# Another order of the outer products in a two-level Strassen-Winograd output stage

## The chip, the cores and the metric

The kernel runs on one core of a Trainium2 chip. The metric is the device time of one execution in microseconds (us); the time before is the median of four runs. A profile of one further execution shows what each engine did: TensorE (PE, with its weight loads as PEld), VectorE (DVE), ScalarE (ACT), GpSimd (POOL), and SyncE (SP), which issues most DMAs.

## The reference

Attention with a hash mask gives x of 3072 x 512 (4 batches x 768 rows, 8 heads x 64). Then a feed-forward block follows, and it is the second product of that block that the change is about:

```python
def _moe_ref(x, w_in, w_out):
    h = x @ w_in                                   # 3072 x 2048
    g = h * (1.0 / (1.0 + np.exp(-1.702 * h)))
    return (g @ w_out).astype(np.float32)          # 3072 x 512
```

All is fp32.

## The kernel before, in words

Attention comes first. Then `feed_forward` computes the hidden layer in a first stage (`hidden`, products of 128x512 at L724) and the outputs in a second stage, which ends the kernel.

Both stages use the Winograd form of Strassen's scheme: a product of 2x2 blocks with seven block products in place of eight, and sums before and after. The output stage uses it twice, one inside the other.

*Outer level.* The tokens lie in three blocks `sb` of 1024. For each block there are seven outer products, numbered 1 to 7, done in the order of the tuple `OUTER`. So the output stage has 3 x 7 = 21 steps, `steps_out`; step n works on `(sb, o)`. `LEFT[o]` names the piece of w_out (or of the sums of its quarters) that the outer product takes, and `RIGHT[o]` the piece of g, which the first stage has left in DRAM (`g_dram`). The result of a step is a tile m of 128 x 4 quarters x 256, kept in `ms[o]`; six places (`wholes`) are used in turn. Some results are added to earlier ones as they are formed: `acc` names the earlier product. Products 6 and 2 take product 1, 7 and 3 take 6, and 4 takes 7. Product 5 takes none; after it, two sums over whole tiles are queued in `pending`, m6 += m5 (L976) and m5 += m7 (L977), and the transposition of m5. Product 3 takes the new m6, so the first of the two sums is done ahead of it.

*Inner level.* `product_of_halves(n, acc, after)` does one step: seven inner products `product(i)`, each four fp32 matmuls (the profile has two records for each), accumulated over four chunks in one of eight PSUM banks (L836); ACT copies the first to u (L849) and the third to c12 (L852), VectorE adds the others (L840). The four quarters c11, c12, c21, c22 of the result form so: the corner c11 = P2 + u, v = P6 + u, c21 = P7 + v, c12 = P3 + v, then P5 is added to c22 and c12, and P4 to c21. Where there is an `acc`, four more adds come in.

*What is put between.* `after(at)` is called at four or five places of a step, and issues work on VectorE in the places that suit it: at 0 whatever waits in `pending`, at 1 to 3 the four sums over g that the next step needs (`g_sums`: t1, b12 in place, t2, t4, at L219 to L222). `inner_sums` forms the sums over the pieces of w_out on POOL; those for the outer steps 5 and 6 are done in the first block ahead of these steps, each behind a copy of one element (`mark`, L940), which makes POOL wait for the corner of the step before:

```python
if n in (5, 6):
    nc.gpsimd.tensor_copy(mark, ms[OUTER[n - 1]][0:1, 0, 0:1])
for f in {0: inner_sums(4), 5: inner_sums(5) + inner_sums(6)[:2], 6: inner_sums(6)[2:]}.get(n, []):
    f()
```

*The outputs.* Finished results are transposed by VectorE, quarter by quarter, into `ys[j]` (`turned(c, i, j, q0, q1)`, L816), and written to DRAM by `written` (L823): four DMAs for one ys, or for a half of it. `ys[0]` needs the products 2 and 4, `ys[1]` the products 5 and 3. While a step runs, SP fetches the pieces of g for steps to come (`fetch`, L791).

*Order.* On PE, VectorE, ACT and POOL, instructions run in the order in which the program issues them. The DMAs on SP's queue are put in order by the framework, and each waits there for its data and its buffer.

Of the kernel before, what the change touches and what calls it, by code (L numbers as in the profile page):

```python
# [38 lines left out]
def kernel(  # L39
# [17 lines left out]
    nc = tc.nc  # L57

    loader = [nc.sync]
# [93 lines left out]
    for x in (0x3FFFFFFF, 0xFF800000):  # L153
        m = const.tile([P, 1], U32, name=f"mask_{x:x}")
# [53 lines left out]
    def sums_a(eng, a11, a12, s3, a22, s1, s2, s4, a21=None):  # L208

        a21 = s3 if a21 is None else a21  # L210
        return [lambda: eng.tensor_tensor(s1, a21, a22, op=Alu.add),
                lambda: eng.tensor_tensor(s3, a11, a21, op=Alu.subtract),
                lambda: eng.tensor_tensor(s2, s1, a11, op=Alu.subtract),
                lambda: eng.tensor_tensor(s4, a12, s2, op=Alu.subtract)]
# [480 lines left out]
    def feed_forward(tag, late=()):  # L695
# [5 lines left out]

        LEFT = dict(zip(range(1, 8), (0, 1, 6, 3, 4, 5, 2)))
        RIGHT = dict(zip(range(1, 8), (0, 2, 3, 6, 4, 5, 1)))
        OUTER = (1, 2, 6, 7, 5, 3, 4)
        with ExitStack() as fctx:
            stage_ctx = fctx.enter_context(ExitStack())
            stage = stage_ctx.enter_context(tc.tile_pool(name=f"stage{tag}", bufs=2, side="right"))
# [4 lines left out]
            def bank():  # L712
                turn[0] += 1
                return sets[turn[0] % 8 // 6 if len(sets) > 1 else 0].tile([P, XT], F32, tag="p", name="product")
# [53 lines left out]
            def w_quarters(o):  # L768

                w = wqs[LEFT[o]]  # L770
                x = [w[:, i, F4 * j : F4 * (j + 1), :] for i in range(2) for j in range(2)]
                at = OUTER.index(o)
                if at == 0:
                    return x[0:2] + rooms[3:4] + x[3:] + rooms[0:3]
                return x + rooms[3 * at + 1 : 3 * at + 4]

            def inner_sums(at):

                if at == 0:
                    w = w_quarters(OUTER[0])  # L780
                    return sums_a(nc.gpsimd, *w, wqs[LEFT[OUTER[0]]][:, 1, 0:F4, :])
                return sums_a(nc.gpsimd, *w_quarters(OUTER[at])) if at < len(OUTER) else []

            steps_out = [(sb, o) for sb in range(n1) for o in OUTER]
            raw_g = [None, s_in[:, 0:2].rearrange("p i k f -> p (i k f)").rearrange("p (c t) -> p c t", t=XT)]
# [25 lines left out]
            def turned(c, i, j, q0, q1):  # L811

                for q in range(q0, q1):
                    h, k = divmod(q, 2)
                    y = ys[j].rearrange("p b (d r) -> p r b d", r=4)[:, 2 * i + h, k * (TH // 32) : (k + 1) * (TH // 32), :]
                    nc.vector.transpose(y, c[:, q].rearrange("p (b t) -> p b t", t=32))  # L816

            def written(sb, j, halves, queues):
                first, last = halves[0] * TH, (halves[-1] + 1) * TH
                for a in range(4):  # L820
                    t0 = (2 * sb + j) * XT
                    dst = out[t0 + first : t0 + last, a * P : (a + 1) * P].rearrange("(b t) d -> t b d", t=32)
                    queues[a % len(queues)].dma_start(out=dst, in_=ys[j][32 * a : 32 * (a + 1), first // 32 : last // 32, :])  # L823

            def product_of_halves(n, acc, after):

                sb, o = steps_out[n]
                wq, gq = w_quarters(o), g_quarters(n)
                m = wholes[n % len(wholes)]
                u, v = (gp.tile([P, TH], F32, tag=x, name=x, bufs=2) for x in ("u", "v"))  # L830
                c11, c12, c21, c22 = (m[:, i] for i in range(4))

                def product(i):
                    ps = bank()[:, 0:TH]
                    for c in range(F4):
                        nc.tensor.matmul(ps, wq[LEFT[i]][:, c, :], gq[RIGHT[i]][:, c, :], start=(c == 0), stop=(c == F4 - 1))  # L836
                    return ps

                def add(dst, x, y):
                    nc.vector.tensor_tensor(dst, x, y, op=Alu.add)  # L840

                def corner():
                    add(c11, product(2), u)
                    if acc is not None:
                        add(c11, c11, acc[:, 0])


                final = n + 1 == len(steps_out)
                nc.scalar.copy(u, product(1))  # L849
                if not final:  # L850
                    corner()
                nc.scalar.copy(c12, product(3))  # L852
                after(0)
                add(v, product(6), u)
                add(c21, product(7), v)
                if acc is not None:
                    add(v, v, acc[:, 1])
                    add(c22, c21, acc[:, 3])
                    add(c21, c21, acc[:, 2])
                add(c12, c12, v)  # L860
                after(1)
                p = product(5)
                add(c22, p, c21 if acc is None else c22)
                add(c12, p, c12)
                after(2)
                if final:
                    corner()
                    after(4)
                add(c21, product(4), c21)
                after(3)  # L870
                return m
# [14 lines left out]
            for sb in range(n1):  # L886
                for mt in range(MT):
                    n = sb * MT + mt
                    if n == 1:
# [12 lines left out]
                        steps = conversions(cv, cps, late + chunks)  # L902
# [31 lines left out]
            for n, (sb, o) in enumerate(steps_out):  # L934
                final = n + 1 == len(steps_out)
                if 0 < n and n + 1 < len(steps_out):
                    fetch(n + 1)
# [5 lines that stand above are left out]
                later_sums = g_sums(n + 1)  # L943
                m = wholes[n % len(wholes)]

                def after(at):
                    if at == 0:
                        while pending:
                            pending.pop(0)()

                    steps = [later_sums[at : at + 1]] if n == 0 else [[], later_sums[0:1], later_sums[1:2], later_sums[2:], []][at : at + 1]

                    if n + 2 >= len(steps_out):
                        turns = [lambda q=q: turned(m, int(final), int(not final), q, q + 1) for q in range(4)]
                        if final:
                            steps = [[[], [], [turns[1], turns[3]], [turns[2]], [turns[0]]][at]]
                        elif at == 3:
                            steps = [later_sums[2:3], turns[0:2], turns[3:4], later_sums[3:], turns[2:3]]
                    for f in sum(steps, []):
                        f()  # L960
                    if final and at in (2, 3):
                        written(sb, 0, (3 - at,), loader + [nc.scalar])
                    if n + 2 == len(steps_out) and at == 3:
                        written(sb, 1, (0, 1), loader + [nc.scalar])

                acc = {6: 1, 7: 6, 2: 1, 3: 6, 4: 7}.get(o)
                if o == 3:
                    pending.pop(0)()
                ms[o] = product_of_halves(n, None if acc is None else ms[acc], after)

                def flat(x):
                    return x.rearrange("p q t -> p (q t)")

                if o == 5:
                    m5, m6, m7 = (ms[i] for i in (5, 6, 7))
                    pending += [lambda a=m6, b=m5: nc.vector.tensor_tensor(flat(a), flat(a), flat(b), op=Alu.add),  # L976
                                lambda a=m5, b=m7: nc.vector.tensor_tensor(flat(a), flat(a), flat(b), op=Alu.add),  # L977
                                lambda a=m5: turned(a, 1, 1, 0, 4)]
                elif o in (2, 3) and n + 2 < len(steps_out):
                    pending.append(lambda a=ms[o], j=int(o == 3): turned(a, 0, j, 0, 4))  # L980
                    if o == 3:
                        pending.append(lambda sb=sb: written(sb, 1, (0, 1), loader))
                elif o == 4 and not final:
                    pending.append(lambda a=ms[4]: turned(a, 1, 0, 0, 4))
                    pending.append(lambda sb=sb: written(sb, 0, (0, 1), loader))
                yield
# [50 lines left out]
```

## Time and profile before

| | us |
|---|---|
| median of 4 runs | 869.91 (869.39 to 870.5) |
| the profiled execution | 869.08 |
| its span, from the first to the last instruction | 867.2 |
| PE busy in it | 856.8 |
| DVE busy in it | 719.2 |
| first matmul of the output stage | 604.38 |
| last matmul ends | 858.77 |
| last transposition on DVE ends | 860.88 |

A line of the timeline has the start in us, the time that it takes in us, the engine, the line of the program, the operation, what it writes from what it reads, shape, and how many instructions are merged in it; in brackets the idle time of the engine before it and what ended that. A line of the chain of work that ended last has the start, the time, and the engine with its line. PEclk is the granted clock of TensorE as a share of full speed (here 0.998 over the span). Offsets such as +3.08 in what follows are us from the first matmul of a step.

### The profile page before, as it was taken

How to read it: one execution, taken by the hardware profiler on the slowest of the kernel's cores; microseconds unless marked ns; L12 is line 12 of the kernel's file. 1: busy time of each engine (PE TensorE's matmuls, PEld its weight loads, DVE VectorE, ACT ScalarE, POOL GpSimd, SP SyncE). 2: the span in 40 equal slices, each digit the busy share in tenths (PEclk: the TensorE clock that was granted, in tenths of full speed). 3: DMA queues.
4: the chain of work that ended last, by engine and by line, in shares of the span. 5: the costliest groups of instructions: out<-in, count | busy, mean ns of one | idle time of the engine just before them, and what ended most of it. 6: DMA issues, size and time to landing. Idle time of an engine off the chain costs nothing.

```text
span 867.2 us, 13473 instructions
## 1 busy us (share of the span) xinstructions
PE 856.8 (99%) x4845; PEld 498.6 (57%) x4845; DVE 719.2 (83%) x1020; ACT 313.4 (36%) x519; POOL 313.5 (36%) x275
## 2 busy tenths in 40 slices
PE   9999999999999999999999999999999999999996
PEld 4444444444444444444444444444888888888885
DVE  4589999999999887778777778888888977897786
ACT  5866667776666642332233322332000000000000
POOL 4242234333223567664544334759904100000000
PEclk9999999999999999999999999999999999999999
DMA  5636645556552205556455555575844685467524
GB/s 133 98 55 108 103 84 85 85 97 118 97 99 60 60 2 195 187 190 216 170 197 190 189 188 195 196 253 179 304 158 153 201 248 196 165 204 243 194 98 100
DMA packets 169162, 132.10 MB, mean 152 GB/s; under 512 B 123616, under 2 KB 138112, under 8 KB 163712
## 3 DMA queue, kind: packets, MB, share of 16 engines
q1 hardware_dynamic: 166528, 129.70, 52.5%
q10 hardware_dynamic: 2560, 1.46, 0.8%
q8 instruction: 40, 0.66, 0.4%
q14 instruction: 34, 0.28, 0.1%
HBM read 79.69 MB, written 50.33 MB: 150 GB/s over the span
## 4 chain that ended last, share of the span: by engine, by line
PE 95%; DVE 3%; issue 0%; DMA 0%; ACTq 0%; ACT 0%; DVEq 0%
PE product L724 33%; PE product L836 26%; PE ps L432 18%; PE av L465 15%; PE dn L486 1%; PE hash L408 1%; DVE y L816 1%; DVE xT L840 1%; PE tp L366 1%; DVE t_x L840 0%; DMA k<-in_k_dram 0%; PE hash L373 0%; DVE t2a L221 0%; DVE raw_g L220 0%; DVE v L840 0%
## 5 line engine op out<-in xcount | busy, mean ns | idle before, releaser
L433 ACT ACTIVATE e<-ps 128x768 f32<-128x768 f32 x192 | 151.3, 812 | 25.6 <-PE ps L432 23.1
L432 PE MATMUL ps<-qT,kT 64*128 64x384 f32 x768 | 155.1, 482 | 0.0
L724 PE MATMUL product<-xT,w_in_sb 128*128 128x512 f32 x288 | 135.4, 592 | 0.0
L465 PE MATMUL av<-e,v 128*32 128x385 f32 x1536 | 128.0, 487 | 0.0
L440 POOL TENSOR_TENSOR acc<-e 128x768 f32<-128x768 f32 x32 | 51.8, 1617 | 193.7 <-ACT e L433 174.2
L732 ACT ACTIVATE c<-c 128x512 f32<-128x512 f32 x72 | 45.4, 630 | 186.7 <-issue 78.6
L724 PEld LDWEIGHTS product<-xT,w_in_sb 128*128 128x128 f32 x288 | 54.6, 190 | 69.0 <-issue 64.5
L465 PEld LDWEIGHTS av<-e,v 128*32 128x32 f32 x1536 | 48.5, 109 | 76.2 <-issue 74.6
L724 PE MATMUL product<-t_x,s_in 128*128 128x512 f32 x192 | 90.2, 592 | 0.0
L432 PEld LDWEIGHTS ps<-qT,kT 64*128 64x128 f32 x768 | 68.0, 187 | 38.5 <-issue 38.4
L219 POOL TENSOR_TENSOR v<-c,u 128x512 f32<-128x512 f32 x24 | 34.2, 1424 | 122.2 <-ACT c L732 122.2
L849 ACT COPY u<-product 128x256 f32<-128x256 f32 x21 | 7.8, 373 | 172.1 <-PE product L836 138.9
L432 PE MATMUL ps<-qf,kf 64*128 64x384 bf16 x384 | 62.8, 324 | 0.1
L724 PEld LDWEIGHTS product<-t_x,s_in 128*128 128x128 f32 x192 | 36.5, 190 | 45.9 <-issue 43.3
L441 POOL TENSOR_TENSOR acc<-acc,e 128x768 f32<-128x768 f32 x32 | 55.8, 1744 | 2.5
L446 DVE SCALAR_TENSOR_TENSOR acc<-e 128x768 f32<-128x768 f32 x32 | 47.7, 1490 | 5.1 <-ACT e L433 5.1
L724 PE MATMUL product<-t_x,w_in_sb 128*128 128x512 f32 x96 | 45.1, 592 | 0.0
L724 PE MATMUL product<-xT,s_in 128*128 128x512 f32 x96 | 45.1, 592 | 0.0
L432 PEld LDWEIGHTS <-kf 64*128 64x128 bf16 x384 | 18.9, 94 | 35.1 <-issue 7.4
L448 DVE TENSOR_TENSOR acc<-acc,e 128x768 f32<-128x768 f32 x32 | 34.3, 1072 | 3.3
L448 DVE TENSOR_TENSOR acc<-acc,acc 128x768 f32<-128x768 f32 x32 | 31.2, 974 | 6.3 <-POOL acc L441 3.2
L836 PE MATMUL product<-raw_g,xT 128*128 128x256 f32 x152 | 35.1, 379 | 0.0
(207 smaller groups left out, 1496.7 us busy)
## 6 DMA issues: line engine op xcount, KB each, us to landing
raw_g<-g_dram SPq DMA_DIRECT2D x22, 1024.0 KB
s_in<-g_dram SPq DMA_DIRECT2D x20, 1024.0 KB
g_dram<-c SPq DMA_DIRECT2D x72, 256.0 KB
g_dram<-t SPq DMA_DIRECT2D x48, 256.0 KB
raw<-in_moe_w_in_dram SPq DMA_DIRECT2D x16, 512.0 KB
raw<-in_moe_w_out_dram SPq DMA_DIRECT2D x16, 512.0 KB
v<-in_v_dram SPq DMA_DIRECT2D x32, 192.0 KB
g_dram<-u SPq DMA_DIRECT2D x24, 256.0 KB
```

What stands on the lines that cost most here:

```text
L219: return [lambda: eng.tensor_tensor(t1, b12, b11, op=Alu.subtract), lambda: eng.tensor_tensor(b12, b22, b12, op=Alu.subtract), lambda: eng ...
L366: nc.tensor.matmul(tp[D * j : D * (j + 1), i * P : (i + 1) * P], x[name][:, j, c * GT + i, :], ident, start=True, stop=True)
L432: nc.tensor.matmul(ps[:, j, 0:HS], a[hs, keys], m[hs, cols], start=not last, stop=last)
L433: nc.scalar.activation(es[c][:, kt, :, 0:HS], ps[:, :, 0:HS], Act.Exp, scale=1.0 / D**0.5)
L440: nc.gpsimd.tensor_tensor(acc, es[c][:, 0, :, 0:HS], es[c][:, 1, :, 0:HS], op=Alu.add)
L441: nc.gpsimd.tensor_tensor(acc, acc, es[c][:, 2, :, 0:HS], op=Alu.add)
L446: nc.vector.scalar_tensor_tensor(acc, e[0], T * TINY, e[1], op0=Alu.add, op1=Alu.add)
L448: nc.vector.tensor_tensor(acc, acc, x, op=Alu.add)
L465: nc.tensor.matmul(av[D * j + d : D * j + d + 32, :], vt[:, t, j, d : d + 32], es[c][:, t, j, :], start=(t == 0), stop=(t == T - 1))
L724: nc.tensor.matmul(ps, wq[LEFT[i]][:, kc, :], xq[RIGHT[i]][:, kc, :], start=(kc == 0), stop=(kc == K2 - 1))
L732: nc.scalar.activation(c, c, Act.Gelu_apprx_sigmoid)
L836: nc.tensor.matmul(ps, wq[LEFT[i]][:, c, :], gq[RIGHT[i]][:, c, :], start=(c == 0), stop=(c == F4 - 1))
```

## The change

The order of the outer products becomes 1, 2, 6, 7, 4, 5, 3. So product 3 is the last of a block, product 4 the fifth and 5 the sixth. In the last block, `ys[0]` (products 2 and 4) is transposed and written from `pending` in the step of product 5, as in the other blocks, and `ys[1]` in two halves in the last step.

The last step of all has its own order of the inner products: it was 1, 3, 6, 7, 5, 2, 4, and becomes 1, 2, 6, 7, 4, 5, 3, where c12 is formed by two adds from P5 + v and P3 and not by ACT's copy of P3. Its quarters are transposed as they are done: c11, c21, then the first half of the rows is written, then c22, c12 and the second half. The special treatment of the step before the last goes: it had transposed and written its own result within the step, partly on ACT's queue.

```diff
-        OUTER = (1, 2, 6, 7, 5, 3, 4)
+        OUTER = (1, 2, 6, 7, 4, 5, 3)
...
                 nc.scalar.copy(u, product(1))
+                corner()
                 if not final:
-                    corner()
-                nc.scalar.copy(c12, product(3))
+                    nc.scalar.copy(c12, product(3))
                 after(0)
                 add(v, product(6), u)
                 add(c21, product(7), v)
...
                     add(c21, c21, acc[:, 2])
+                if final:
+
+                    add(c21, product(4), c21)
+                    after(1)
+                    p = product(5)
+                    add(c22, p, c22)
+                    after(2)
+                    add(c12, p, v)
+                    add(c12, product(3), c12)
+                    after(3)
+                    return m
                 add(c12, c12, v)
                 after(1)
                 p = product(5)
                 add(c22, p, c21 if acc is None else c22)
                 add(c12, p, c12)
                 after(2)
-                if final:
-                    corner()
-                    after(4)
                 add(c21, product(4), c21)
                 after(3)
                 return m
...
-                    if n + 2 >= len(steps_out):
-                        turns = [lambda q=q: turned(m, int(final), int(not final), q, q + 1) for q in range(4)]
-                        if final:
-                            steps = [[[], [], [turns[1], turns[3]], [turns[2]], [turns[0]]][at]]
-                        elif at == 3:
-                            steps = [later_sums[2:3], turns[0:2], turns[3:4], later_sums[3:], turns[2:3]]
+                    if final:
+                        turns = [lambda q=q: turned(m, 0, 1, q, q + 1) for q in range(4)]
+                        steps = [[[turns[0]], [turns[2]], [turns[3]], [turns[1]]][at]]
                     for f in sum(steps, []):
                         f()
-                    if final and at in (2, 3):
-                        written(sb, 0, (3 - at,), loader + [nc.scalar])
-                    if n + 2 == len(steps_out) and at == 3:
-                        written(sb, 1, (0, 1), loader + [nc.scalar])
+                    if final and at in (1, 3):
+                        written(sb, 1, (at // 2,), loader + [nc.scalar])
...
-                elif o in (2, 3) and n + 2 < len(steps_out):
+                elif o in (2, 3) and not final:
                     pending.append(lambda a=ms[o], j=int(o == 3): turned(a, 0, j, 0, 4))
                     if o == 3:
                         pending.append(lambda sb=sb: written(sb, 1, (0, 1), loader))
-                elif o == 4 and not final:
+                elif o == 4:
                     pending.append(lambda a=ms[4]: turned(a, 1, 0, 0, 4))
                     pending.append(lambda sb=sb: written(sb, 0, (0, 1), loader))
```

## The prediction

> **What bounds the kernel now.** I read the page first: the span, the engines' shares, the chain that ended last by engine.
>
> ```profile
> span 867.2 us, 13473 instructions
> PE 856.8 (99%) x4845; PEld 498.6 (57%) x4845; DVE 719.2 (83%) x1020; ACT 313.4 (36%) x519; POOL 313.5 (36%) x275
> PE 95%; DVE 3%; issue 0%; DMA 0%; ACTq 0%; ACT 0%; DVEq 0%
> ```
>
> TensorE sets the time. The change takes no matmul away, so it can gain only where TensorE stands still, or behind its last matmul. The chain in order of time shows where, in the stage of the outputs:
>
> ```profile
> 681.13 1.14 DVE t2a L221
> 682.28 0.14 issue
> 682.41 160.83 PE product L836 x744
> ...
> 853.83 0.38 ACT u L849
> ...
> 860.25 0.63 DVE y L816
> ```
>
> At 682.41 TensorE has waited for the sum t2a; from there it runs without a break; from about 854 the chain is on VectorE. A product of halves (8 matmul records) takes 1.725 us, a step of seven 12.09 (822.35 to 834.43). The step that starts at 676.93 is followed by one at 689.39, 12.46 later: the stall is 0.37. It is the only one of that size: the other thirteen steps to 846.52 take 157.13, 12.087 each. The timeline shows a step's VectorE work, and the tail:
>
> ```profile
> 834.43 3.62 PE L836 MATMUL product<-s_in,xT 128*128 128x256 f32 x16
> 837.51 1.22 DVE L976 TENSOR_TENSOR t_x<-t_x,xT 128x1024 f32<-128x1024 f32 x1
> 838.65 0.42 DVE L840 TENSOR_TENSOR xT<-product,u 128x256 f32<-128x256 f32 x1
> 839.44 1.22 DVE L977 TENSOR_TENSOR xT<-xT,t_x 128x1024 f32<-128x1024 f32 x1
> 840.70 2.06 DVE L816 STREAM_TRANSPOSE y<-xT 128x256 f32<-128x256 f32 x4
> 842.57 0.44 DVE L840 TENSOR_TENSOR v<-product,u 128x256 f32<-128x256 f32 x1
> ...
> 854.24 0.42 DVE L840 TENSOR_TENSOR v<-product,u 128x256 f32<-128x256 f32 x1 [1.49 <-ACT u L849]
> 856.88 1.89 PE L836 MATMUL product<-t4g,w_out_sb 128*128 128x256 f32 x8
> 860.25 0.63 DVE L816 STREAM_TRANSPOSE y<-xT 128x256 f32<-128x256 f32 x1
> ```
>
> TensorE ends at 858.77, VectorE at 860.88: VectorE is late by 1.0 against the least possible (one add of 0.42 and one transpose of 0.63 behind the last matmul). Behind it the output's bytes drain (stretches of 1 us; the last two columns are DMA share and GB/s):
>
> ```profile
> 859.00:860.00 1.00, 0.00 (x0) 0.00 (x0) 0.97 (x3) 0.00 (x0) 0.00 (x0) 1.00 0.64 130
> 861.00:862.00 1.00, 0.00 (x0) 0.00 (x0) 0.00 (x0) 0.00 (x0) 0.00 (x0) 1.00 1.02 262
> 863.00:864.00 1.00, 0.00 (x0) 0.00 (x0) 0.00 (x0) 0.00 (x0) 0.00 (x0) 0.93 1.01 223
> 864.00:865.00 1.00, 0.00 (x0) 0.00 (x0) 0.00 (x0) 0.00 (x0) 0.00 (x0) 0.50 0.65 133
> ```
>
> The queues are full from about 859.3 to 864.7; the span ends 2.5 later.
>
> **Part 1: outer products 4, 5, 3 for 5, 3, 4.** Each step keeps its 56 matmul records, so TensorE's work is unchanged: 0. What moves is VectorE's work. Outer product 3 is the heavy step: L976, L977, four transposes and four more adds with the earlier product (acc). Before, the light 5 precedes it; after, 5 still does, but carries product 4's four transposes (2.06 by the row at 840.70). Cover: in the step from 822.35, product 5 before, VectorE waits 2.35 ahead of v and 1.30 ahead of the next add. After an acc step its corner add comes at +4.34 (826.69 against 822.35), so the transposes run from +4.7 to +6.75, before product 6 lets v start at +7.10. They cost nothing; without that cover they would cost up to 2.06 at VectorE. The heavy step then begins as now: L976 at +3.08 (837.51 against 834.43).
>
> In the first block the stall arises because the heavy step's predecessor is stretched by POOL: L219 takes 2.29 at 663.09 and L220 1.63 at 665.97, against 1.22 each elsewhere. POOL's sums of outer steps 5 and 6 follow a one-element copy (L940) that waits for the previous product's corner. That copy's first wait now includes an acc add (+0.45, from 657.58), its second loses L976 and an acc add (from 672.31 to about 671.4). So the stretched sums stay in the step from 652.75 to 664.84, but what follows is the light 5, not the heavy 3. Working through the DVE rows, t2a for the step from 676.93 is ready at about 679.7, needed at 682.1; the next heavy step gives its successor's t2a at 693.0, needed at 694.2. The stall goes: -0.37 (bounds: 0 if POOL's two remaining sums stretch other adds, -0.40 with the 0.03 at 633.73).
>
> GPSIMD Engine Reference of the Trainium skill, section 1 (Specifications), says that POOL shares its SBUF interface with VectorE, in contention with instructions that have two SBUF inputs. The rows at 663.09 and 665.97 agree; by this rule alone the two sums from 671.4 would stretch any two-input add they meet, 1 us or so each, an estimate from 2.29 less 1.22. Beside the transposes (one input) the row at 673.42 shows none: 2.07 against 2.06.
>
> DMA queue: product 4's write of y (four issues on SP, 3.38 to 3.42 in all at 686.29 and 696.61) moves from the next block's first step to step 5, past the fetch for two steps on. The second half of that fetch, issued at 673.67, would go at about 677 to 678; L219 reads it at about 688.4 (688.55 now). The nearest row: issued at 689.81 for a read at 698.90, 9.1 us, with no wait there. Here 10.4 remain: 0. If it were late, the price is bounded by one issue stretch, 3.4. Product 3's write then takes the place of product 4's in the next block's first step: 0.
>
> **Part 2: the next to last step.** Its own four transposes and its half of the output (four issues, two on ACT) go. They hold ACT from 840.1 to 853.74, which delays u (L849) to 853.83 and VectorE by 1.49. Now ACT copies u at about 848.3. That wait goes; what is late next is VectorE's own queue. Half of the last 2 MB (y0, 1 MB) now leaves from about 841 instead of 852.8.
>
> **Part 3: the last step.** It is now heavy: P1, P2, P6, P7, P4, P5, P3. VectorE enters at 846.52 + 3.08 = 849.60. Spacings from the rows above and the tail's rows: L976 1.14; corner 0.45 + 0.34; L977 1.26; four transposes 1.87; the corner's own transpose 0.48; v 0.53, c21 0.46, v 0.34, c22 and c21 0.80 (0.40 each), P4 0.45; transpose 0.48; P5 0.45 (its wait on the sum included), transpose 0.48, c12 0.45, P3 0.45, last transpose 0.63. The sum is 11.06: the end is at 860.7, against 860.88. No product is late: P4 is done at 855.2 and needed at 857.2, P3 at 858.6 and needed at 859.6. So -0.2 (bounds: -1.0 if VectorE kept up with TensorE; +1.3 if the step were entered like an acc step's corner, at +4.35).
>
> **Part 4: the drain.** 2 x 512 KB, as now; the first half goes after the second own transpose, about 858.4 (858.62 now), the second at 860.7 (860.91 now): the same gap of 2.3. The rest of the earlier 1 MB no longer sits in front. I take no more than the shift; the bound is the rate: 1 MB in 5.4 us now, 4.7 at the row's 223 GB/s, so -0.7. DMA: Bandwidth & Descriptors, section "Anatomy of one DMA", puts a fixed cost of about 2.0 us on a transfer, mostly the write's receipt. By it the end would follow only the last issue; the windows show full queues until 864.7, so the first half's issue counts as much.
>
> **Sum.** -0.37 - 0.2 - 0 = -0.55: span 866.65, the profiled execution 869.08 - 0.55 = 868.5. The median shown, 869.91, is 0.83 above the profiled execution: 869.3.
>
> **Rivals.**
> - *Slower: VectorE enters the last step late.* Place: v of the next to last step. If the 2.35 + 1.30 of waits there were used up, the 2.06 of transposes and the 1.27 between +4.35 and +3.08 would add up to 3.3 on a tail that has nothing to absorb it: +2.75, 872.7. It decides from 2.3 on. For it: the last step holds 11.1 us of VectorE work in a 12.09 step. Against: those waits stand in the profile.
> - *Faster: TensorE sets the tail.* If adds go closer than I chain them, the end is 858.4 + 1.05, -1.4 against 860.88, and with -0.5 of the drain 868.0.
> - *Nothing comes of it.* POOL's sums stretch the next step, the stall stays, and the last step ends where it did: between -0.2 and +0.9, about 870.2.
>
> **How the numbers follow.** A measurement of this kernel tells about 0.2% (1.74 us) from no change. Forecast (-0.2 to -1.4): 0.52, same. Nothing: 0.22, same. Faster rival: 0.15. Slower rival: 0.11. Together: faster 0.15, same 0.74, slower 0.11. The range leaves out most of the slower rival and half of the faster one: 868.0 to 870.8.
>
> **What would show it.** Right: steps of 12.09 throughout, no break of TensorE near 682; no wait of VectorE for ACT's u in the last step; y0 written from 841; VectorE's last transpose ends at 860.2 to 860.5, and 1.6 to 2.0 after TensorE. Wrong: a break of TensorE near 682 or 694, L976 in the last step later than +3.5, a gap between the adds of the last step that is longer than 0.6, or SP's fetch late for L219.

## The result, and the profile after

The changed kernel takes 870.59 us (median of 32 runs) against 869.87 for the kernel before (52 runs): 1.0010 of its time, 95% interval 1.0005 to 1.0015. The ratio is taken over all runs and is not the quotient of the two medians, which would be 1.0008. So the kernel is slower by 0.7 us, where -0.6 was forecast. The interval does not reach 1, though the move is under the 0.2% that the prediction took for the least that can be told. The profiled execution took 869.83, its span 868.0.

The page after (the span, the engines' busy times, and the chain that ended last by engine):

```profile
span 868.0 us, 13477 instructions
PE 856.9 (99%) x4845; PEld 498.3 (57%) x4845; DVE 720.4 (83%) x1020; ACT 313.1 (36%) x518; POOL 311.9 (36%) x275
PE 96%; DVE 3%; issue 0%; POOL 0%; DVEq 0%; POOLq 0%
```

TensorE's work is the same to 0.1 us; the page doesn't tell where the time went. The chain in order of time does (start, us, engine, line):

```profile
661.43 0.44 DVE t_x L840
...
662.31 1.42 DVE t_x L840
...
663.75 2.78 DVE t_x L840 x2
...
669.80 1.14 DVE t2b L221
670.94 0.14 issue
671.08 172.92 PE product L836 x800
```

Before, the chain left VectorE for TensorE at 682.41, behind t2a. Now it does so at 671.08, behind t2b, one step earlier. From there TensorE has no break any more: every later step takes 12.08 or 12.09. The timeline at that place, POOL included:

```profile
661.43 0.42 DVE L840 TENSOR_TENSOR t_x<-product,v 128x256 f32<-128x256 f32 x1 [1.30 <-PE product L836]
661.92 1.51 POOL L214 TENSOR_TENSOR w_in_sb<-xT,w_in_sb 128x512 f32<-128x512 f32 x1
662.23 2.90 DVE L840 TENSOR_TENSOR t_x<-t_x,xT 128x256 f32<-128x256 f32 x2
663.39 1.45 POOL L211 TENSOR_TENSOR w_in_sb<-xT 128x512 f32<-128x512 f32 x1
664.68 3.62 PE L836 MATMUL product<-s_in,xT 128*128 128x256 f32 x16
664.92 1.33 POOL L212 TENSOR_TENSOR xT<-xT 128x512 f32<-128x512 f32 x1
665.04 1.48 DVE L840 TENSOR_TENSOR t_x<-t_x,v 128x256 f32<-128x256 f32 x1
666.45 1.21 DVE L219 TENSOR_TENSOR t1b<-s_in 128x1024 f32<-128x1024 f32 x1
669.72 1.21 DVE L221 TENSOR_TENSOR t2b<-s_in,t1b 128x1024 f32<-128x1024 f32 x1
671.08 1.97 PE L836 MATMUL product<-t2b,w_in_sb 128*128 128x256 f32 x8 [1.05 <-DVE t2b L221]
678.06 3.62 PE L836 MATMUL product<-raw_g,xT 128*128 128x256 f32 x16
```

The same place in the kernel before, from the add of product 7 to the product that takes t2b:

```profile
661.59 0.42 DVE L840 TENSOR_TENSOR t_x<-product,v 128x256 f32<-128x256 f32 x1 [1.30 <-PE product L836]
667.85 1.21 DVE L221 TENSOR_TENSOR t2b<-s_in,t1b 128x1024 f32<-128x1024 f32 x1
670.02 1.89 PE L836 MATMUL product<-t2b,w_in_sb 128*128 128x256 f32 x8
```

Two adds that take 0.88 elsewhere take 2.90 beside POOL's sums, a third takes 1.48 in place of 0.42. Everything behind them on VectorE moves, and TensorE waits 1.05 for t2b, which was ready 0.96 before it was wanted (669.06 against 670.02) in the kernel before. The sixth step lasts from 664.68 to 678.06, 13.38, where 12.09 is usual: +1.29. The seventh has its usual length, so the old stall of 0.37 is gone. From the first matmul of the stage (604.21, 604.38 before) to that of the last step (847.27, 846.52 before) the balance is +0.92.

The tail, as offsets from the first matmul of the last step:

| | before | after |
|---|---|---|
| v starts | +7.72 | +8.62 |
| last transposition ends | +14.36 | +14.36 |
| span ends | +20.66 | +20.75 |

```profile
855.89 0.40 DVE L840 TENSOR_TENSOR v<-product,u 128x256 f32<-128x256 f32 x1
861.00 0.63 DVE L816 STREAM_TRANSPOSE y<-xT 128x256 f32<-128x256 f32 x1
```

VectorE does not wait for ACT's u any more (no bracket at v), but it gets to v later, with its own queue, and ends at the same distance. So the loss lies in the first block.

### The profile page after: what moved, and what is told of

It reads as the page before. It is cut to its first block, busy times and chain, and to the rows that moved or that the text cites. A ratio compares the mean times of both kernels' runs of the same rounds, so it can differ in the third digit from the quotient of the medians.

```text
span 868.0 us, 13477 instructions
## 1 busy us (share of the span) xinstructions
PE 856.9 (99%) x4845; PEld 498.3 (57%) x4845; DVE 720.4 (83%) x1020; ACT 313.1 (36%) x518; POOL 311.9 (36%) x275
## 4 chain that ended last, share of the span: by engine, by line
PE 96%; DVE 3%; issue 0%; POOL 0%; DVEq 0%; POOLq 0%
PE product L724 33%; PE product L836 26%; PE ps L432 18%; PE av L465 15%; PE dn L486 1%; PE hash L408 1%; DVE t_x L840 1%; DVE xT L840 1%; PE tp L366 1%; DVE y L816 1%; PE hash L373 0%; DVE t4g L222 0%; DVE raw_g L220 0%; DVE xT L979 0%; DVE t2b L221 0%
## 5 line engine op out<-in xcount | busy, mean ns | idle before, releaser
L219 POOL TENSOR_TENSOR v<-c,u 128x512 f32<-128x512 f32 x24 | 34.2, 1423 | 122.3 <-ACT c L732 122.3
```

The costliest lines, as they stand in the source:

```text
L219: return [lambda: eng.tensor_tensor(t1, b12, b11, op=Alu.subtract), lambda: eng.tensor_tensor(b12, b22, b12, op=Alu.subtract), lambda: eng ...
```

## The experiments

Theory A: POOL's sums behind the first mark stretch VectorE's adds in the fifth step; the new order has four more adds there (the acc adds), and t2b is late for the sixth step. Rival B: the four adds alone make it late. Rival C: the loss lies in the tail.

**Two of the six sums moved behind the second mark** (`e1_split`):

```diff
-for f in {0: inner_sums(4), 5: inner_sums(5) + inner_sums(6)[:2], 6: inner_sums(6)[2:]}.get(n, []):
+for f in {0: inner_sums(4), 5: inner_sums(5), 6: inner_sums(6)}.get(n, []):
```

> The changed kernel with one edit: of POOL's six sums that follow the first mark, the last two (for the seventh step) are put behind the second mark, so four stand there. Theory A (POOL's sums stretch VectorE's two-input adds of the fifth step, which the new order has more of, and t2b for the sixth step comes too late): without the two sums the two adds of c22 and c21 take under 1.8 us where they took 2.90, the add of c12 0.42 to 0.9 where it took 1.48, t2b is ready before TensorE wants it at about 669.9, TensorE's break of 1.05 is gone, and the time falls by 0.9 to 1.3 against the changed kernel: 869.3 to 869.7. Rival B (the three more adds alone make VectorE late, POOL adds little): the break stays at over 0.7, the time at 870.2 to 870.8. Rival C (the loss is in the last step's tail): the break may go, the time stays at 870.4 or more.

Measured: 869.38 against 870.02 for the kernel before measured beside it, ratio 0.9992 (0.9983 to 1.0000). Its timeline (the profiled execution was 3.5 us late before it came to this stage, so only distances count):

```profile
665.74 1.95 DVE L840 TENSOR_TENSOR t_x<-t_x,xT 128x256 f32<-128x256 f32 x2
667.61 0.42 DVE L840 TENSOR_TENSOR t_x<-t_x,v 128x256 f32<-128x256 f32 x1
671.21 1.21 DVE L221 TENSOR_TENSOR t2b<-s_in,t1b 128x1024 f32<-128x1024 f32 x1
673.37 1.89 PE L836 MATMUL product<-t2b,w_in_sb 128*128 128x256 f32 x8
```

t2b is ready at 672.42, 0.95 ahead of TensorE, and there is no break. The two adds took 1.95, a little over the 1.8 expected. The time is 1.36 lower than the changed kernel's, each against its own kernel before (-0.64 and +0.72), and the intervals of the two ratios do not meet. B and C fall: the acc adds and the new tail are all still there. The two sums that were moved do stretch VectorE in the sixth step (an add of 0.42 takes 0.98, L219 2.29), but there t2a is still ready at 683.82 and TensorE takes it at 685.46.

**One sum moved** (`e7_one_sum`; the same edit with `[:1]` and `[1:]`):

> The changed kernel, with five POOL sums behind the first mark in place of six (none moved: 1.05 break; two moved: t2b ready 0.95 ahead). Theory A, each sum costs VectorE the time for which it holds the common reads, about 1.0 us: t2b comes within 0.3 of the time at which TensorE wants it, so a break of 0 to 0.3. A rival in which any overlap at all sets VectorE back by a fixed amount: the break is still 1.0.

```profile
662.99 2.90 DVE L840 TENSOR_TENSOR t_x<-t_x,xT 128x256 f32<-128x256 f32 x2
665.81 0.41 DVE L840 TENSOR_TENSOR t_x<-t_x,v 128x256 f32<-128x256 f32 x1
670.77 1.97 PE L836 MATMUL product<-t2b,w_in_sb 128*128 128x256 f32 x8
```

The add of c12 (665.81), which took 1.48 in the changed kernel, has its usual time again. t2b ends at 670.63, and TensorE starts 0.14 late (a product of 1.725 behind 668.90 would be 670.63). The single run took 869.70.

The price goes with the number of sums that VectorE's adds meet, and the changed kernel's timeline shows it one for one. POOL's fourth, fifth and sixth sum end at 663.43, 664.84 and 666.25, and the three stretched adds, taken singly, at 663.72, 665.12 and 666.53, each 0.28 or 0.29 behind a sum. POOL's first three sums, from 658.01 to 661.84, met only two adds that read PSUM, at 0.42 each.

**No sums behind the first mark, and the changed kernel again beside it** (`e8_no_sums`, `e9_changed_again`). The first leaves out the six sums, so the products of the sixth and seventh steps take unsummed pieces and its outputs are not those of the reference:

```diff
-for f in {0: inner_sums(4), 5: inner_sums(5) + inner_sums(6)[:2], 6: inner_sums(6)[2:]}.get(n, []):
+for f in {0: inner_sums(4), 6: inner_sums(6)[2:]}.get(n, []):
```

> The changed kernel without the six sums over w_out that POOL forms behind the first mark (left out of the computation, so the products of the sixth and seventh steps take unsummed pieces); the fifth step keeps its four acc adds on VectorE. Theory A (POOL's sums and the acc adds together make t2b late): from the add of product 7 in the fifth step to the end of t2b pass 6.4 us, as in an acc step without POOL, no break, 1.1 to 1.4 below the changed kernel of the same call. Rival B (the acc adds alone): 8.5 or more from that add to t2b, the break stays.

> The changed kernel itself, for a comparison on one chip with the run without the sums. Theory A: again a break of 1.0 to 1.1 in the sixth step, 9.4 to 9.6 us from the add of product 7 in the fifth step to the end of t2b, and 0.5 to 1.0 above the kernel before. If the break were an accident of one execution, it is not there again, or of another size.

Without the sums: 869.43, ratio 0.9995 (0.9986 to 1.0004). The changed kernel: 870.65, ratio 1.0013 (1.0004 to 1.0021), with the break again, of 1.06. Leaving out the sums saves 1.22. Without the sums the two adds take what they take elsewhere:

```profile
663.18 0.88 DVE L840 TENSOR_TENSOR t_x<-t_x,xT 128x256 f32<-128x256 f32 x2
667.58 1.22 DVE L221 TENSOR_TENSOR t2b<-s_in,t1b 128x1024 f32<-128x1024 f32 x1
```

The runs together give the sum that the prediction should have had. It goes from the start of product 7's add in the fifth step to the end of t2b; TensorE wants t2b 8.43 after that start (669.86 in the changed kernel):

| fifth step | distance | against 8.43 |
|---|---|---|
| light, no POOL beside it (831.18 to 836.34, kernel before) | 5.16 | |
| with acc adds, no POOL (`e8_no_sums`) | 6.42 | 2.01 to spare |
| light, six sums (kernel before) | 7.47 | 0.96 to spare |
| acc adds, four sums (`e1_split`) | 7.48 | 0.95 to spare |
| acc adds, five sums (`e7_one_sum`) | 8.43 | none to spare |
| acc adds, six sums (changed kernel) | 9.50 | 1.07 late |

The acc adds cost 1.26 (three of the four lie in this stretch), POOL's six sums 3.08 beside them: the first four 1.06 together, the fifth 0.95, the sixth 1.07. Neither alone breaks TensorE.

**The order of the first block by itself, both ways.** In `e2_old_first` the changed kernel keeps the old order in the first block; in `e3_new_first` the kernel before has the new order in the first block and the old one in the others:

```diff
 # e2_old_first
-OUTER = (1, 2, 6, 7, 4, 5, 3)
-steps_out = [(sb, o) for sb in range(n1) for o in OUTER]
+OUTER = (1, 2, 6, 7, 5, 3, 4)
+steps_out = [(sb, o) for sb in range(n1) for o in (OUTER if sb == 0 else (1, 2, 6, 7, 4, 5, 3))]
 # e3_new_first, in the kernel before
-OUTER = (1, 2, 6, 7, 5, 3, 4)
-steps_out = [(sb, o) for sb in range(n1) for o in OUTER]
+OUTER = (1, 2, 6, 7, 4, 5, 3)
+steps_out = [(sb, o) for sb in range(n1) for o in (OUTER if sb == 0 else (1, 2, 6, 7, 5, 3, 4))]
```

> The changed kernel, but the first of the three blocks in the order of before (1, 2, 6, 7, 5, 3, 4); the blocks 2 and 3 and the tail are as changed. Theory A: the break of TensorE is again the small one of before, 0.3 to 0.4 ahead of the seventh step's product 6, and the time is that of before, 869.6 to 870.0. Rival C (the tail or the order in the later blocks loses): 870.4 to 870.8, as the changed kernel.

> The kernel before, but the first block alone in the new order (1, 2, 6, 7, 4, 5, 3); blocks 2 and 3 and the tail are as before. Theory A: TensorE breaks for 1.0 to 1.3 in the sixth step and the time is 0.7 to 0.9 above before: 870.6 to 870.8. Rival C: 869.7 to 870.1.

Measured, with the kernel before at 870.02: 870.10 (1.0001, 0.9992 to 1.0009) and 870.73 (1.0011, 1.0000 to 1.0021). The first has the time of the kernel before and its small stall (its seventh step takes 12.47), the second that of the changed one, with the same break (1.06, 9.51 from add to t2b). So the blocks 2 and 3 and the new tail are worth nothing that these intervals show, and the first block accounts for the difference.

**The tail: ACT freed in the kernel before** (`e4_act_free`):

```diff
-    written(sb, 1, (0, 1), loader + [nc.scalar])
+    written(sb, 1, (0, 1), loader)
```

> The kernel before with the next to last step's four output DMAs all on SP's queue, none on ACT's, so that ACT copies u at once. If VectorE's end sets the tail, v starts about 1.4 earlier, VectorE ends at about 859.9 (860.88 before) and the time falls by 0.8 to 1.0: 868.9 to 869.1. If the draining of the last 2 MB sets it, VectorE ends as early, but the DMA queues are full until 864.2 to 864.7 all the same, and the time falls by 0 to 0.5: 869.4 to 869.9.

Measured: 869.37 against 870.02, ratio 0.9993 (0.9984 to 1.0001). The last line is a stretch of 1 us, with DMA share and GB/s at its end:

```profile
853.76 0.40 DVE L840 TENSOR_TENSOR v<-product,u 128x256 f32<-128x256 f32 x1
860.42 0.63 DVE L816 STREAM_TRANSPOSE y<-xT 128x256 f32<-128x256 f32 x1
864.00:865.00 1.00, 0.00 (x0) 0.00 (x0) 0.00 (x0) 0.00 (x0) 0.00 (x0) 0.50 0.67 145
```

With the last step at 847.68 here, v starts at +6.08 and VectorE ends at +13.37, 1.0 earlier than before; the queues are still two thirds busy between +16.3 and +17.3. The span ends at +20.16, 0.5 earlier. The measured 0.65 lies between the two expectations, and its interval covers both. The run does not part them, and the trace shows one reason: ACT issues its two writes of the last half at +13.40, but SP, which by the profile waited 2.2 for an earlier write, issues its two at 862.17, +14.49, no earlier than before (860.91, +14.39). So VectorE's earlier end did not reach half of the last writes.

**The tail: VectorE relieved in the changed order** (`e5_pool_last`, on top of `e1_split`):

```diff
 # in after(0)
+if n + 2 == len(steps_out):
+    nc.gpsimd.tensor_copy(mark, m[0:1, 0, 0:1])
+    for f in g_sums(n + 1, nc.gpsimd)[0:2]:
+        f()
 # in after(at), before the case of the last step
+if n + 2 == len(steps_out):
+    steps = [[[], [], later_sums[2:3], later_sums[3:]][at]]
```

> The changed kernel with POOL's sums split over both marks (as in the run of that name) and one more edit: in the next to last step, behind its corner, POOL forms the first two of the four sums over g for the last step (t1 and b12); VectorE keeps t2 and t4. If VectorE's backlog at the start of the last step sets the tail (theory D), L978 starts at about +1.7 of the last step where it started at +3.1, VectorE ends at +13.0 to +13.4 where it ended at +14.36, limited now by TensorE's last product, and the time falls by 0.9 to 1.3 below the split kernel: 868.1 to 868.5. If the draining of the output sets it (rival E), VectorE ends as early, the time falls by less than 0.5: 868.9 or more. If POOL's two sums stretch VectorE's adds as they did in the first block, L978 comes no earlier than +2.6 and the gain is under 0.5 too.

Measured: 869.16 against 869.34, ratio 0.9997 (0.9988 to 1.0006): no gain that shows over the split alone. The first sum of the last step (m6 += m5) starts at +1.75, as theory D has it. But then the corner waits for product 2:

```profile
850.37 0.43 DVE L840 TENSOR_TENSOR xT<-product,u 128x256 f32<-128x256 f32 x1 [0.76 <-PE product L836]
859.90 0.63 DVE L816 STREAM_TRANSPOSE y<-xT 128x256 f32<-128x256 f32 x1
```

VectorE ends at +13.9 and not at +13.0 to +13.4: 0.5 of the 1.3 is left, and of this nothing shows in the time. Rival E's number came in, but D was not given a fair trial, since VectorE's end moved by half of what was meant.

**The old order mended** (`e6_before_mended`: ACT free, and POOL's marks in the steps 5 and 6 counted from one, not 6 and 7):

```diff
-if n in (5, 6):
+if n in (4, 5):
-for f in {0: inner_sums(4), 5: inner_sums(5) + inner_sums(6)[:2], 6: inner_sums(6)[2:]}.get(n, []):
+for f in {0: inner_sums(4), 4: inner_sums(5), 5: inner_sums(6)}.get(n, []):
-    written(sb, 1, (0, 1), loader + [nc.scalar])
+    written(sb, 1, (0, 1), loader)
```

> The kernel before in its old order, with two edits: the next to last step's output DMAs on SP alone (as in the run with ACT free), and POOL's sums for the sixth and seventh step one step earlier each, behind the corners of the fourth and the fifth step, so that the second four lie in the light step of product 5. Theory A: the break of 0.37 goes, the time is 0.3 to 0.4 below the run with ACT free: 868.9 to 869.1. Rival: four sums in the fourth step (with its four acc adds) stretch VectorE there and a break of more than 0.3 comes one step earlier: 869.3 or more.

Measured: 868.93 against 869.34, ratio 0.9993 (0.9984 to 1.0002). TensorE has no break in the stage:

```profile
682.45 1.89 PE L836 MATMUL product<-t2a,s_in 128*128 128x256 f32 x8
```

It starts 1.73 behind the product before it (680.72), with t2a ready at 682.16. The expected time was met, but the kernel before took 869.34 here and 870.02 beside the run with ACT freed, and the ratio is that of ACT freed alone; the 0.37 can be seen in the trace only. `e1_split`, `e4_act_free` and this kernel have the lowest ratios, 0.9992 and 0.9993, and the interval of each still reaches 1.0000: none of them is shown to be faster than the kernel before.

## Why the prediction was wrong

The sign was wrong, by one term. The time still fell in the predicted range, 868.0 to 870.8, but not for a reason that the prediction gave: its sum stood at 869.3, and the range was wide enough for a stall that it had not seen. Point by point:

- **The old stall (-0.37): right.** t2a for the seventh step ends at 680.04, predicted 679.7, and TensorE takes it at 683.24. `e1_split`, where no break comes ahead of that step, shows it better: no step of the stage takes more than 12.13.
- **The step that failed** is in part 1: "So the stretched sums stay in the step from 652.75 to 664.84, but what follows is the light 5, not the heavy 3." What the prediction works out from it is only t2a, the sum that the seventh step wants. It does not ask for t2b of the sixth step itself, which is wanted earlier. The rows for it were there: t2b ended at 669.06 before (667.85 + 1.21) and TensorE took it at 670.02, 0.96 later. The new order puts product 4, with its acc adds, in the place of the light 5, so that POOL's sums meet two-input adds of 128x256 where they had met L219 and L220. That takes 2.03 more (9.50 less 7.47) out of 0.96, so t2b is 1.07 late. The measured price is +1.29 on the sixth step, the lateness and 0.22 until TensorE is back at its pace; the prediction had 0.
- **The rule on the shared interface was weighed at the wrong place.** What GPSIMD Engine Reference of the Trainium skill, section 1, says of instructions with two SBUF inputs was set against the two sums behind the second mark, with an estimate of 1 us for each. Those sums ran from 672.73 to 675.35, beside transpositions and adds that read PSUM. They met one add of two SBUF operands only in their last 0.16 (675.19, 0.45), and L219 began behind them (675.56, 1.21). But the same rule with the same estimate, for two sums behind the first mark, is what was measured: 8.43 less 7.48 and 9.50 less 8.43, 0.95 and 1.07 for each.
- **SP's queue (0): right.** The second half of the fetch went out at 678.38 (predicted 677 to 678), and L219 read it at 688.82 without a wait.
- **The next to last step: right.** ACT copies u at 849.24, +1.97 in the last step, and VectorE does not wait for it; the first write of y goes out at 841.92.
- **The last step (-0.2): mis-sized, measured 0.0.** VectorE reached v at +8.62, as predicted. Product 4's add came at +10.90 (predicted +10.75), the last transposition at +13.73 (predicted +13.51): the two acc sums ahead of product 4's add took 0.98 where 0.80 was taken, and product 3's add came 0.51 behind the add whose result it reads, where 0.45 was taken.
- **The drain (0): right**, 6.39 from VectorE's end to that of the span, 6.30 before. The fixed cost of 2.0 us that the prediction cites from "Anatomy of one DMA" is given there for DMAs issued by GpSimd, while these writes were issued by SP and ACT; no term of the sum rests on it.
- **The rivals.** None was this one. The slower rival had the right kind (VectorE late, and nothing to absorb it), but in the last step; there VectorE came in at +3.08 as forecast. "Nothing comes of it" had POOL's sums stretch the next step, and came near in time (870.2), but kept the old stall and did not have the new one. The list of signs named a break near 682 or 694; it came at 671.
- **The sum.** Its terms add up to -0.57, where -0.55 is written; nothing hangs on it.

## What to carry to other kernels

When work changes places, list every deadline between the old place and the new one, not only the one that was late before: here the next engine's wait one step earlier had 0.96 us to spare, and the row for it was in the trace. Here POOL's sums cost nothing beside transpositions and adds from PSUM, and about 1 us each where they met adds of two SBUF operands; if an order is changed, what runs beside such sums must be looked up again.

## What the runs showed of the hardware

- In these traces POOL and VectorE held each other up only at VectorE's instructions with two operands in SBUF: two adds of 128x256 took 2.90 in place of 0.88, L219 2.29 in place of 1.22, while transpositions (2.05 against 2.06) and adds from PSUM (0.42) kept their times. POOL's sums beside them took 1.33 to 2.14 in place of 1.27. By the spans of the profile an add of 128x256 that began during a POOL sum of 128x512 ended 0.28 or 0.29 behind it (three in the changed kernel), so the fifth and the sixth sum cost VectorE about 1.0 us each, and the first three, which met no such add, nothing.
- That price came back with the same size each time: 9.50, 9.51 and 9.51 from product 7's add to t2b in the changed kernel, in `e3_new_first` and in `e9_changed_again`.
- The issue of an output write on SP grew from 0.34 to 0.48, 1.01 and 1.43 us over four in a row of 256 KB (`e4_act_free`), so SP was held for 3.4 us.
- What ends the span behind VectorE is not settled. From its end to that of the span pass 6.3 to 6.9 us in the profiles of kernels where VectorE ends at about +14.4 (6.30 before, 6.39 after, 6.90 in `e2_old_first`), and 6.55, 6.79 and 7.28 in those with an earlier end (`e5_pool_last`, `e4_act_free`, `e6_before_mended`). In the last two, SP issued its last writes 1.1 and 1.4 behind VectorE's end. In all the traces the last bytes of the output land 2.2 to 3.0 ahead of the span's end (864.71 before, 865.62 after), so part of the spread lies behind them. With that spread a gain of 0.5 at VectorE's end can't be followed to the end of one profiled execution; what fills the time behind the last bytes was not tried.
